# Attention stage rebuilt: one read of V with a shifted copy, 32x32 turns on DVE, the maximum subtracted on PE

## The chip, the cores and the metric

The kernel runs on one core of a Trainium2 chip. A core has five engines with their own instruction streams: PE (matrix multiply, with weight loads), DVE (vector), ACT (scalar functions), POOL (general, here mostly the issue of DMAs) and SP (issue of DMAs); 16 DMA engines move data between DRAM and the on-chip memory SBUF. PE writes to a memory of its own, PSUM, which DVE and ACT read. The metric is the device time in microseconds, the median of the runs; lower is better.

## The reference

Two layers follow each other. First an attention by chunks over q, k, v of shape 4 x 8 x 768 x 64 (batch, head, row, width): each chunk of 32 query rows sees 16 rows to its left, its own 32, 8 to its right, and 8 memory rows of its head, 64 keys in all.

```python
for c in range(nc):                       # 24 chunks of 32 rows
    l_start, r_end = max(0, 32*c - 16), min(S, 32*c + 32 + 8)
    k_full = concat(mem_k, k[l_start:r_end]); v_full = concat(mem_v, v[l_start:r_end])
    scores = (q_c @ k_full.T) / sqrt(64)
    a = exp(scores - max(scores)); a = a / (sum(a) + 1e-9)
    out_c = a @ v_full
```

Its output, 3072 tokens of 512, goes into a mixture of 8 experts: logits and noise logits per token, the two best experts with a softmax over the two, and for each the product `relu(x @ w1[e]) @ w2[e]` (512 to 1024 to 512), weighted and added.

## The kernel before

**Pairs, batches, groups.** The attention runs over 16 head pairs (`NPAIR`; four per batch). A loop of 19 iterations (lines 479 to 519) is a software pipeline written out by hand. Its order is the order of each engine's queue. In iteration i, PE transposes P of pair i-1 (`PT_pe`), multiplies pair i-3 by the router's weights (`logits_pe`), transposes q and k of pair i+2 (`qkT_pe`, 24 matmuls against an identity in four PSUM tiles, evacuated by ACT in four copies), multiplies P of pair i-1 with V (`PV_pe`), makes the scores of pair i+1 (`scores_pe`) and transposes the output of pair i-2 (`xT_pe`). DVE takes the maximum of pair i (`max_dve`), copies the transposed P of pair i-1 from PSUM (`PT_dve`), subtracts the maximum (`sub_dve`, whose exponential is ACT's) and divides the output of pair i-1 (`mult_dve`). The score tile `ps_s` and the output tile `ps_o` have one buffer each, so scores of i+1 wait until those of i have been read, and PV of i-1 waits for `mult_dve` of i-2.

**Scores and PV.** The scores of a pair lie as 128 query rows (four chunks) by six blocks `u` by 64 keys; one bank for each head. `scores_pe` takes 12 matmuls for the memory keys and 48 of 64 rows by 32 columns for the windows. `PV_pe` takes six matmuls of 128 x 128 for the memory rows and a column of ones (which gives the sum for the division), then 24, one per chunk, of 128 rows by 32 columns for both heads together.

**Loads.** All of q, k, v is loaded by POOL, with a cast from fp32 to bf16, in groups of two pairs, three groups deep. V is stored by chunk: 56 partitions hold the window rows of a chunk, so rows that lie in two windows are read twice, in runs of one row (`load_v`, line 121). Loads of a later group stand in the loop behind the work that frees the buffer, and on POOL's queue in the order of the program, among the scatters named next.

**Routing.** When the four pairs of a batch are through the logits, `start_route` puts the route of the batch into a list, of which `steps` runs one entry per iteration: `s1` and `s2` (choice of two experts), then `s3` to `s6`, `s7(0)` and `s7(1)` (each six indirect DMAs on POOL, which scatter the rows of `xrow` with their gates into per-expert lists in DRAM, line 420), and `s8`. Batches 0, 1 and 2 are routed inside the loop, in iterations 7, 11 and 15; batch 3 after it.

**Experts.** From iteration 16 SP loads the rows of the lists transposed (`load_x`; it waits for the scatters of batch 2), and PE runs the up and down products of the eight experts (lines 529 to 701). The results are gathered, added and scattered to the output by indirect DMAs on POOL. An expert list holds up to 832 rows; a loop for rows beyond that is in the program and is not entered by this data.

**Start.** DVE clears three V buffers and `zrow`; ACT issues eight DMAs that write zeros to the ends of the lists, then the four that load `mk_nat` (the memory keys), whose transposes are PE's first work (line 224).

## Time and profile before

| | us |
|---|---|
| runs of the kernel | 442.45, 445.95, 452.03 |
| median | 445.95 |
| profiled execution: its time | 448.12 |
| its span, first to last instruction | 446.4 |
| mean granted PE clock | 0.818 |
| busy: PE, DVE, ACT, POOL | 288.7, 175.6, 108.0, 219.9 |

Lines of the profile name an engine, a line of the kernel, an operation and its tiles (out<-in) with count, busy time and the mean of one in ns, and the idle time before them with what ended it. In the order of time a row begins with its start and its length in us and ends with the idle time before it in brackets; "issue" is idle time for which the profile shows no semaphore. Rows of stretches give start and end, length, busy us of PE, its weight loads, DVE, ACT and POOL, then the granted PE clock, the DMA share and the GB/s moved, counted as written. The strips on the page cut the span in 40 slices of 11.2 us, in tenths.

### The profile page before, as it was taken

What the parts mean: (1) busy time and instruction counts of PE and PEld (TensorE: products, weight loads), DVE (VectorE), ACT (ScalarE), POOL (GpSimd) and SP (SyncE); (2) the same over time, 40 slices, a digit from 0 to 9 for tenths busy, and PEclk for the clock granted to TensorE, in tenths of its full rate; (3) what the DMA queues carried; (4) which work ended last, traced back from release to release, by engine and by line L of the source; (5) the groups of instructions that cost most, each with busy time, mean ns of one, the idle gap of its engine ahead of it and who ended that gap; (6) DMA issues with size and microseconds to landing.
All of it is one profiled execution on the core that took longest, in us unless ns stands there. A gap on an engine that the chain in (4) does not pass through costs nothing. (4 is left out here: it accounts for less than half of the span.)

```text
span 446.4 us, 7962 instructions
## 1 busy us (share of the span) xinstructions
PE 288.7 (65%) x3247; PEld 168.7 (38%) x3257; DVE 175.6 (39%) x403; ACT 108.0 (24%) x202; POOL 219.9 (49%) x245
## 2 busy tenths in 40 slices
PE   0077686527646550595780599869887888979950
PEld 0065565315535430242340254335442443435420
DVE  7234566505632752050220262534623526345230
ACT  1064564306523221142140013013030030301300
POOL 7952341587364036037347152734726717456660
PEclk9998885658555655598895699889998998999995
DMA  9999999139994012515869997595995965943440
GB/s 82 206 167 153 145 107 67 65 100 160 164 212 156 1 46 106 100 42 141 211 141 145 197 209 229 106 245 125 162 222 151 161 182 130 245 128 142 131 159 33
DMA packets 121640, 63.36 MB, mean 142 GB/s; under 512 B 93516, under 2 KB 110940, under 8 KB 121600
## 3 DMA queue, kind: packets, MB, share of 16 engines
q0 software_dynamic: 81488, 54.22, 74.1%
q1 hardware_dynamic: 38672, 7.41, 9.7%
q10 hardware_dynamic: 1440, 1.18, 0.9%
q8 instruction: 27, 0.44, 0.4%
q14 instruction: 13, 0.11, 0.1%
HBM read 69.79 MB, written 21.43 MB: 204 GB/s over the span
## 5 line engine op out<-in xcount | busy, mean ns | idle before, releaser
L604 PE MATMUL ps_y<-w2t,ht 128*128 128x512 bf16 x375 | 92.5, 403 | 31.5 <-DMA w2t<-in_moe_w_dram 17.8
L590 POOL DMA_INDIRECT acc<-out_dram,gi x49 | 49.9, 1018 | 64.1 <-issue 60.2
L555 PEld LDWEIGHTS <-w1t 128*128 128x128 bf16 x512 | 50.9, 101 | 75.9 <-issue 39.2
L612 POOL DMA_INDIRECT out_dram<-acc,wi x56 | 55.9, 998 | 44.7 <-DVE acc L610 20.7
L555 PE MATMUL ps_g<-xT,w1t 128*128 128x416 bf16 (+2 forms) x280 | 64.6, 346 | 13.2 <-issue 6.4
L604 PEld LDWEIGHTS <-ht 128*128 128x128 bf16 x384 | 39.3, 103 | 82.8 <-issue 42.4
L555 PE MATMUL ps_h<-xT,w1t 128*128 128x416 bf16 (+2 forms) x231 | 58.6, 359 | 16.7 <-DMA xT<-x_lists 13.2
L610 DVE SCALAR_TENSOR_TENSOR acc<-ps_y,mt,acc 128x512 f32<-128x512 f32 (+1 forms) x49 | 34.0, 695 | 63.4 <-PE ps_y L604 37.9
L420 POOL DMA_INDIRECT x_lists<-xrow,offA x24 | 23.9, 996 | 60.7 <-issue 25.4
L543 ACT ACTIVATE ht<-ps_g 128x416 bf16<-128x416 f32 (+2 forms) x44 | 21.9, 511 | 115.8 <-PE ps_g L555 69.4
L121 POOL DMA_DIRECT2D vg<-in_v_dram x34 | 33.0, 976 | 27.9 <-PE ps_o L307 20.9
L543 ACT ACTIVATE ht<-ps_h 128x416 bf16<-128x416 f32 (+2 forms) x41 | 21.5, 532 | 77.3 <-issue 35.7
L545 DVE TENSOR_SCALAR ht<-ps_g 128x416 bf16<-128x416 f32 (+2 forms) x26 | 15.0, 579 | 38.9 <-PE ps_g L555 27.1
L420 POOL DMA_INDIRECT x_lists<-xrow,offB x24 | 23.9, 996 | 10.8 <-issue 5.5
L265 PE MATMUL ps_s<-kT,qT 64*32 64x56 bf16 (+2 forms) x768 | 14.8, 213 | 21.5 <-issue 20.9
L276 DVE TENSOR_REDUCE mx<-ps_s 128x12 f32<-128x768 f32 x16 | 15.2, 951 | 30.8 <-PE ps_s L268 30.8
L331 ACT COPY xt<-p_x 128x768 bf16<-128x768 bf16 x16 | 12.8, 799 | 54.8 <-PE p_x L329 53.9
L563 DVE MEMSET acc<- 128x512 f32 x49 | 23.8, 485 | 2.9 <-issue 0.3
L243 ACT CAST qT<-p_t 128x384 bf16<-128x384 f32 x32 | 17.2, 596 | 18.0 <-PE p_t L241 17.1
L265 PEld LDWEIGHTS <-qT 64*32 64x32 bf16 x768 | 10.3, 99 | 24.5 <-issue 24.2
L319 DVE RECIPROCAL rec<-ps_o 128x12 f32<-128x12 f32 x16 | 3.7, 233 | 38.7 <-PE ps_o L307 21.7
L243 ACT CAST kT<-p_t 128x384 bf16<-128x384 f32 x32 | 17.1, 612 | 4.7 <-PE p_t L241 4.6
(128 smaller groups left out, 329.2 us busy)
## 6 DMA issues: line engine op xcount, KB each, us to landing
w1t<-in_moe_w_dram POOLq DMA_DIRECT2D x8, 1024.0 KB
w2t<-in_moe_w_dram POOLq DMA_DIRECT2D x8, 1024.0 KB
vg<-in_v_dram POOLq DMA_DIRECT2D x30, 168.0 KB
qg<-in_q_dram POOLq DMA_DIRECT2D x6, 384.0 KB
kg<-in_k_dram POOLq DMA_DIRECT2D x6, 384.0 KB
x_lists<-zrow ACTq DMA_DIRECT2D x8, 136.0 KB
out_dram<-acc,wi POOLq DMA_INDIRECT x56
acc<-out_dram,gi POOLq DMA_INDIRECT x49
```

What stands on the lines that cost most here:

```text
L121: nc.gpsimd.dma_start(out=vg[p0 + j:p0 + j + nj, x, c:c + n, hh, :], in_=bass.AP(v.tensor, v.offset + (hd * S + c * chunk + j - left_ctx) ...
L243: nc.scalar.copy(dst[:, :, SH * x:SH * (x + 1)], p_t.rearrange("d j p -> d p j"))
L265: nc.tensor.matmul(out=o[:, lo:hi], lhsT=qT[hs, chunk * c:chunk * (c + 1)], rhs=kT[hs, k0 + lo:k0 + hi], start=True, stop=True)
L276: nc.vector.tensor_reduce(out=mx, in_=st[n]["ps"], axis=AX, op=Alu.max)
L420: sc = nc.gpsimd.indirect_dma_start(out=xl_part[2 * (t0 + t) + role], out_offset=bass.IndirectOffsetOnAxis(ap=R["off"][role][:, t:t + 1], ...
L543: nc.scalar.activation(out=dst, in_=src, func=Act.Relu)
L555: nc.tensor.matmul(out=ps[x][:, :w], lhsT=W1[e][:, kp, f * 128:(f + 1) * 128], rhs=XT[e][:, kp, lo + x * w:lo + (x + 1) * w], start=(kp == ...
L563: nc.vector.memset(a, 0.0)
L590: nc.gpsimd.indirect_dma_start(out=(a[:, :DH] if last else a).bitcast(I32), out_offset=None, in_=(out_h(out) if last else out).bitcast(I32 ...
L604: nc.tensor.matmul(out=ps_y, lhsT=HT[e][:, f, i * 128:(i + 1) * 128], rhs=W2[e][:, f, :], start=(f == 0), stop=(f == FB - 1))
L610: nc.vector.scalar_tensor_tensor(out=a[:, :w], in0=ps_y[:, :w], scalar=gate, in1=a[:, :w], op0=Alu.mult, op1=Alu.add)
L612: nc.gpsimd.indirect_dma_start(out=out_h(o) if last else o, out_offset=bass.IndirectOffsetOnAxis(ap=IX[e][0][:, i:i + 1], axis=0), in_=a[: ...
```

## The change

The attention stage and its loads are rebuilt; from the logits on, the code is the same, with other line numbers.

- **Layout of keys.** The 64 keys of a chunk are ordered as two halves (even and odd rows) of 28 window positions and 4 memory positions each. V is loaded once per batch into `va`, two rows of V to a partition, 128 partitions a tile, 24 tiles a batch; `vb` is the same shifted by 16 partitions (32 rows), made from `va` by DMAs inside SBUF (`spread_v`, on SP). In both, partitions 28 to 31 of every 32 are overwritten with memory rows from `memst`. A chunk's window then lies in 32 partitions of `va` (even chunks) or `vb` (odd chunks). Columns of ones stand to the left and right of the two rows.
- **Chunks to rows.** The rows of a score tile are chunks `8*(s//2) + 2*r + s%2`, so tokens stand in another order in `xrow`; the noise and the token numbers (`nz_all`, `tok_i`, `part_i`, `tile_i`) are loaded or made in that order.
- **Scores.** Two matmuls per chunk and head (memory 2 x 4 keys, window 2 x 28), 96 a pair, all 64 rows by 32 columns. The maximum is written as bf16 and subtracted by PE: two matmuls of 384 columns with minus the identity add it into the score banks; ACT's exponential reads PSUM.
- **P.** DVE turns P in 32 x 32 blocks in SBUF (`PT_dve`); the six PE transposes and the copy are gone.
- **PV.** 96 matmuls a pair of 32 rows by 32 columns against 65 columns of `va` or `vb`, for each half j; the sum of exponentials is the sum of columns 0 and 65 of each block (a small reduce before the reciprocal).
- **Turns of q and k.** Transposes with bf16 output in one PSUM tile of six, evacuated by one ACT copy each; q's is placed ahead of the maximum's subtraction, k's behind it.
- **Order.** Loads by whole batches, two deep, on POOL: batch 0 in two parts, batch 1 in the prologue, batches 2 and 3 in iterations 2 and 4, 6 and 8. `s7(0)` and `s7(1)` are taken out of the list and put behind `steps`, in iterations 7, 11, 15 and 8, 12, 16. w1 of expert 0 is loaded in iteration 8, w2 of expert 0 in 9, w1 of expert 1 in 12. The zero writes and DVE's constants move into `constants()` in iteration 2, on SP; `mk_nat` is loaded first on ACT's queue.

```diff
...
+        VP, V0 = 160, 16
+        VT = H * S // 256
+        vbufs = [(ap_.tile([128, VT + 1, VP], BF16, name=f"va{i}", bufs=1), ap_.tile([128, VT, VP], BF16, name=f"vb{i}", bufs=1)) for i in range(2)]
...
+        def load_v(b, lo, hi):
+            va, at = vbufs[b % 2][0], v.offset + (b * H * S - left_ctx) * D
...
+            nc.gpsimd.dma_start(out=va[:, lo:hi, V0:V0 + 2 * D], in_=bass.AP(v.tensor, at + 256 * lo * D, [[2 * D, 128], [256 * D, hi - lo], [1, 2 * D]]))
...
+        def spread_v(b, lo, hi):
+            va, vb = vbufs[b % 2]
+            nc.sync.dma_start(out=vb[:112, lo:hi, :], in_=va[16:, lo:hi, :])
+            nc.sync.dma_start(out=vb[112:, lo:hi, :], in_=va[:16, lo + 1:hi + 1, :])
+            for dst in (va, vb):
+                for r in range(4):
+                    nc.sync.dma_start(out=dst[32 * r + 28:32 * r + 32, lo:hi, :], in_=memst[4 * b:4 * b + 4, lo:hi, :])
...
+        load_qk(0, 0, 2)
...
+        load_v(0, 0, 7)
...
+        nc.scalar.copy(memst.rearrange("p (h r) c -> p h r c", h=H)[:, :, :, V0:V0 + 2 * D],
+                       mv_nat.rearrange("p h (o c) -> p h o c", o=1).to_broadcast([B * 4, H, VT // H, 2 * D]))
+        load_qk(0, 2, H)
+        load_v(0, 7, VT)
+        spread_v(0, 0, 6)
...
+        spread_v(0, 6, VT)
...
+        load_qk(1)
+        load_v(1, 0, VT)
+        spread_v(1, 0, VT)
...
+        def constants():
+            for e in range(E):
+                nc.sync.dma_start(out=xl_d[(e + 1) * CAP - 128:(e + 1) * CAP, :], in_=zrow)
...
+        def turn_pe(n, x):
...
+            p_t = psT.tile([128, SJ, 128], BF16, name="p_t", tag="tr")
+            for j in range(SJ):
+                for hh in range(2):
+                    nc.tensor.transpose(out=p_t[64 * hh:64 * hh + 64, j, :], in_=src[:, 2 * hp + hh, j * D:(j + 1) * D], identity=identb)
...
+                nc.scalar.copy(dst.rearrange("d (p j) -> d j p", j=SJ), p_t)
...
-        def sub_dve(n):
-            sd = ap_.tile([128, 2, BT, CTX], F32, name="sd")
-            nc.vector.tensor_tensor(out=sd, in0=st[n]["ps"], in1=bc4(st[n]["mx"], CTX), op=Alu.subtract)
+        def sub_pe(n):
+            for hh in range(2):
+                nc.tensor.matmul(out=st[n]["ps"][:, hh], lhsT=minus, rhs=st[n]["mx"][:, hh, :].rearrange("p (s o) -> p s o", o=1).to_broadcast([128, BT, CTX]),
+                                 start=False, stop=True, skip_group_check=True)
...
-            for u in range(BT):
-                nc.tensor.transpose(out=p_p[:, u, :], in_=P[:, u, :, :], identity=identb)
...
-            nc.vector.tensor_copy(PT, st[n]["p_p"])
+            PT = ap_.tile([128, BT, 2, 2, 32], BF16, name="PT")
+            nc.vector.transpose(out=PT.rearrange("p s h j c -> p (s h j c)"), in_=st[n]["P"].rearrange("p s h c -> p (s h c)"))
...
+            for s in range(BT):
+                for hh in range(2):
+                    t = (2 * hp + hh) * (VT // H) + s // 2
+                    for j in range(2):
+                        for r in range(4):
+                            rs = slice(32 * r, 32 * r + 32)
+                            nc.tensor.matmul(out=po[rs, hh, s * OW + j:s * OW + j + D + 1], lhsT=PT[rs, s, hh, j, :],
+                                             rhs=vbufs[b % 2][s % 2][rs, t, V0 - 1 + j * (D + 1):V0 + D + j * (D + 1)],
+                                             start=(s == 0 and j == 0), stop=(j == 1), skip_group_check=True)
...
+            if i + 2 < NPAIR:
+                turn_pe(i + 2, 0)
             if i < NPAIR:
                 max_dve(i)
+                sub_pe(i)
             if i + 2 < NPAIR:
-                qkT_pe(i + 2)
+                turn_pe(i + 2, 1)
...
+            steps(1)
+            if i in (2, 6):
+                load_qk(i // 4 + 2)
+            if i in (4, 8):
+                load_v(i // 4 + 1, 0, VT)
+                spread_v(i // 4 + 1, 0, VT)
+            if i in (7, 11, 15):
+                done[i // 4 - 1]["s7"](0)
+            if i == 8:
                 load_w1(0)
+            if i == 9:
                 load_w2(0)
+            if i == 12:
                 load_w1(1)
-            steps(1)
+            if i in (8, 12, 16):
+                done[i // 4 - 2]["s7"](1)
```

## The prediction

> **What bounds the kernel now.** I read the page first, for the stages.

> ```profile
> span 446.4 us, 7962 instructions
> ...
> PEclk9998885658555655598895699889998998999995
> DMA  9999999139994012515869997595995965943440
> ...
> q8 instruction: 27, 0.44, 0.4%
> ...
> L604 PE MATMUL ps_y<-w2t,ht 128*128 128x512 bf16 x375 | 92.5, 403 | 31.5 <-DMA w2t<-in_moe_w_dram 17.8
> ...
> vg<-in_v_dram POOLq DMA_DIRECT2D x30, 168.0 KB
> qg<-in_q_dram POOLq DMA_DIRECT2D x6, 384.0 KB
> ```

> One slice is 11.2 us. For seven slices the DMA engines are full while PE's clock flips between half and full; then comes a hole, a second load burst, and from slice 17 the experts. Then the order of time, from which the pace is read: PE's first work, one maximum per head pair (pairs 0, 2, 5, 6, 8, 9, 12, 13, 15), the third batch's scatter (first and last of 12), and the first expert matmul.

> ```profile
> 23.23 0.60 PE L224 MATMUL p_m<-ident,mk_nat 32*128 32x32 f32 x4 [23.23 <-DMA mk_nat<-in_mem_k_dram]
> 27.01 0.96 DVE L276 TENSOR_REDUCE mx<-ps_s 128x12 f32<-128x768 f32 x1 [12.99 <-PE ps_s L268]
> 37.58 0.95 DVE L276 TENSOR_REDUCE mx<-ps_s 128x12 f32<-128x768 f32 x1
> 58.11 0.95 DVE L276 TENSOR_REDUCE mx<-ps_s 128x12 f32<-128x768 f32 x1
> 63.14 0.95 DVE L276 TENSOR_REDUCE mx<-ps_s 128x12 f32<-128x768 f32 x1
> 81.19 0.95 DVE L276 TENSOR_REDUCE mx<-ps_s 128x12 f32<-128x768 f32 x1
> 99.60 0.96 DVE L276 TENSOR_REDUCE mx<-ps_s 128x12 f32<-128x768 f32 x1 [11.95 <-PE ps_s L268]
> 123.28 0.95 DVE L276 TENSOR_REDUCE mx<-ps_s 128x12 f32<-128x768 f32 x1
> 134.58 0.96 DVE L276 TENSOR_REDUCE mx<-ps_s 128x12 f32<-128x768 f32 x1 [3.53 <-PE ps_s L268]
> 153.85 0.95 DVE L276 TENSOR_REDUCE mx<-ps_s 128x12 f32<-128x768 f32 x1
> 161.78 0.98 POOL L420 DMA_INDIRECT x_lists<-xrow,offA  x1 [17.16 <-DVE base L431]
> 176.28 0.98 POOL L420 DMA_INDIRECT x_lists<-xrow,offB  x1 [0.31 <-issue]
> 183.31 0.58 PE L555 MATMUL ps_h<-xT,w1t 128*128 128x512 bf16 x1 [13.22 <-DMA xT<-x_lists]
> ```

> Four things. PE starts at 23.23, waiting for mk_nat, whose DMAs stand behind eight zero writes on ACT's queue. Pairs 2 to 6 take 25.6 us, 6.4 each; the undisturbed step 58.11 to 63.14 takes 5.0. Two steps are far longer: 18.4 and 11.3 us. And attention hands over through one chain: the scatter of batch 2 begins 7.9 us after the last maximum, lasts 15.5, and 6 us later the experts start. Their 263 us are untouched. So what attention gains or loses by pair 15 reaches the end one for one. The long steps are read next:

> ```profile
> 82.05 1.12 POOL L420 DMA_INDIRECT x_lists<-xrow,offA  x1 [12.80 <-issue]
> ...
> 87.83 0.27 PE L265 MATMUL ps_s<-kT,qT 64*32 64x56 bf16 x5 [1.16 <-issue]
> ...
> 96.39 0.98 POOL L420 DMA_INDIRECT x_lists<-xrow,offB  x1 [0.30 <-issue]
> ...
> 111.22 0.50 PE L265 MATMUL ps_s<-kT,qT 64*32 64x56 bf16 x43 [2.08 <-issue]
> ```

> While Pool scatters (82.05 to 97.4), PE gets its matmuls in handfuls with gaps of 1.2 us that no semaphore explains, until the maximum of 99.60, about 2 us after the scatter. Elsewhere there are single gaps, as the 2.1 us at 111.22. As built, PE's program has 7,211 rows and the instruction queue moved 27 packets: one per 267 rows. A pair issues 272 rows, and such a gap comes at most once in a pair. I take both kinds to be PE waiting for its program, whose packets pass the same DMA engines.

> **The change part by part.** Prices of one operation:

> ```profile
> L281 DVE TENSOR_TENSOR sd<-ps_s,mx 128x768 f32<-128x768 f32 x16 | 15.2, 948 | 0.0
> L295 DVE COPY PT<-p_p 128x768 bf16<-128x768 bf16 x16 | 8.8, 551 | 1.4 <-PE p_p L290 1.4
> L320 DVE TENSOR_TENSOR xrow<-ps_o,rec 128x768 bf16<-128x768 f32 x16 | 15.3, 957 | 1.1 <-POOL xrow L315 0.4 <-DVE rec L319 0.2
> L319 DVE RECIPROCAL rec<-ps_o 128x12 f32<-128x12 f32 x16 | 3.7, 233 | 38.7 <-PE ps_o L307 21.7 <-remote 13.9 <-PE p_x L329 3.1
> L243 ACT CAST qT<-p_t 128x384 bf16<-128x384 f32 x32 | 17.2, 596 | 18.0 <-PE p_t L241 17.1 <-issue 0.9
> L331 ACT COPY xt<-p_x 128x768 bf16<-128x768 bf16 x16 | 12.8, 799 | 54.8 <-PE p_x L329 53.9 <-PE p_p L290 0.9
> ...
> 59.65 0.53 PE L241 MATMUL p_t<-identb,qg 128*64 128x128 bf16 x12
> 61.43 0.52 PE L307 MATMUL ps_o<-vg,PT 128*32 128x128 bf16 x24
> 62.17 0.51 PE L265 MATMUL ps_s<-kT,qT 64*32 64x56 bf16 x40
> 73.36 0.99 PE L241 MATMUL p_t<-identb,kg 128*64 128x128 bf16 x12 [0.36 <-ACT qT L243]
> 75.98 0.83 PE L307 MATMUL ps_o<-vg,PT 128*32 128x128 bf16 x24
> ...
> 10.00:20.00 10.00, 0.00 (x0) 0.00 (x0) 3.48 (x19) 0.00 (x0) 8.09 (x10) 1.00 1.31 194
> 23.20:80.00 56.80, 42.63 (x1163) 34.64 (x1164) 29.78 (x52) 31.33 (x59) 20.62 (x24) 0.82 1.62 123
> ```

> *Start and loads.* mk_nat goes ahead of the zero writes, which move to SP at pair 2, behind the copies; PE can then begin near 12 us (the va memsets, and the ACT copy that fills memst, stand before it). That lead does not last. Pair 2's iteration opens with transposes of pair 4, which need q and k of batch 1. One tensor's batch is 0.79 MB in bf16 (8 heads x 768 x 64 x 2 B). Ahead stand q, k, v of batch 0, the copy vb with its memory rows (1.2 MB) and q, k of batch 1: 5.1 MB. At 123 and at 194 GB/s (last column) that is 26 to 42 us. V's runs double in length and V falls from 5.4 MB (30 issues of 168 KB, the first and the last head's beside them) to 3.1, so I take 185: 28 us plus 2 before the first issue. Pair 2 at 30 instead of 37.6: **-7.6**, range -9 to +6.

> *The pair.* DVE loses the 0.95 subtraction and the 0.55 copy and gains a transpose of 768 elements and a small reduce (0.23, as the reciprocal). No row shows the transpose. The copy of the same tile, 0.55, bounds it below; above I allow the reduce with half as much again, 1.4; I take the 0.95 of the reduce, which also walks 768 elements one by one. DVE: 3.64 to 3.3 us. ACT evacuates q and k in two copies of about 0.9 (row L331, some more for the stride) instead of four of 0.6, and reads the scores from PSUM for the exponential; it stays below 4 us. PE's 24 PV matmuls of 128 columns, four beside each other, took 0.52 at full clock (row 61.43, "warm") and 0.83 at half (75.98, "cold"); six over the full width stream as many columns and cost the same. So before, PV (six and 24) and six transposes each of P and xT cost four times that. Now PV is 96 of 65 columns, each worth 0.51 (columns) to 0.61 (with the 32 weight columns) of one of the 24: 1.1 to 1.3 us warm, 1.7 to 2.0 cold. The transposes of P go. Scores become 96 instead of 60, at 40 in 0.51 less the last one's passage of some 0.15 (an estimate): 0.85 instead of 0.55. Subtracting the maximum costs two of 384 columns; L604's 375 of 512 took 0.25 each, so 0.37 warm, 0.7 cold. With the 24 q and k transposes (1.06 warm, 1.7 cold without the tails) PE's work beside the logits is 4.0 us warm (3.7 before) and 6.0 cold (5.6). Order matters more: the subtraction no longer covers PV on DVE. The loop is maximum 0.95, transpose 0.95, PV 1.2, reduce, reciprocal and product 1.42, hand-overs 0.3 (an estimate): 4.8; through PE 4.0 plus the logits, which wait for the copy of xt (0.8): 4.9. So **4.9 us** against 5.0, range 4.5 (a 0.55 transpose) to 7.0 (all at half clock, 6.0 plus 1.0). From pair 2 to 6 the load pace goes too: 25.6 us become 4 x 5.1 plus what follows, 22.6: **-3**, range -7 to +6. For the nine steps after pair 6, about 0.4 each off the loaded, half-clock ones: **-4**, range -9 to +15.

> *PE's program.* It grows to 10,347 rows: 12 more packets, 464 rows or 1.7 packets a pair. A boundary costs between nothing and the 2.1 us of 111.22; about half of the added ones fall in loaded time. I take 0.8 for five: **+4**, from 0 to 12 x 2 = 24. [...]

> *Scatters.* The step of 18.4 us and the three from 123.28 to 153.85 take 49 us, some 25 more than four at 6. Now the two roles of batches 0 and 1 are scattered an iteration apart, with load_v(3) and load_w1(0) in front of the second; load_v(3) waits for PV of pair 7, which is in PE's slow time. More program per pair means that PE runs dry sooner in each window: **+2**, from -6 to +10. In exchange no q, k or V load stands behind a scatter any more. Batch 2's scatter now overlaps the last PV (192 rows), covered by the chain above that waits for the scatter anyway; uncovered it would be 3.

> *Moved at no cost:* constants() puts 11 DVE operations of some 0.2 us and eight zero writes into pair 2, where PE waits for q and k; the writes stand on SP behind spread_v(1) and must only precede the first scatter. SP's eight noise pieces and ten copies per piece of V are waited for only by PV and the route of pair 6; PV(0) may wait for them, hidden by the 30 us. W1 and W2 are issued earlier, the experts need them after 160 us.

> **Sum:** -7.6 - 3 - 4 + 4 + 2 = -8.6. The profiled execution took 448.1 us (446.4 span and 1.7 around it), the median of the runs is 446.0; I put the sum on the median: **437 us**.

> **The rivals.**

> A, a *larger gain* (423). PE becomes denser, keeps full clock, the transpose is as cheap as the copy, the program gaps go with the load. Start -9, pairs 2 to 6 -7, then -7: -23. For it: 5.0 us in a stretch at full clock. Against: loads last until pair 8 in both.

> B, *no net change* (446). The start lead is real but boundaries (+8) and scatter windows (+6) take it back; the same stall, later.

> C, *slower: PE becomes the bound at half clock* (461). A pair then costs PE 7.0 us with the logits' wait, against 6.4 in the four loaded steps and 5.4 in nine (the undisturbed 5.0, and some allowance for half clock). It decides from about 5.7 us a pair on: 4 x 0.6 + 9 x 1.6 = +17, program +4, scatter +2, start -7.6: +15. The clock decides:

> ```profile
> 100.07 0.85 PE L290 MATMUL p_p<-identb,P 128*128 128x128 bf16 x6
> ...
> 99.60:103.10 3.50, 3.19 (x42) 2.61 (x40) 2.38 (x3) 1.90 (x4) 3.50 (x6) 0.51 1.18 175
> 103.10:106.50 3.40, 2.79 (x116) 2.30 (x116) 2.12 (x4) 2.37 (x4) 3.34 (x4) 1.00 2.17 148
> ```

> A full window (3.19 of 3.50 busy) brings the clock from 0.51 to 1.00, and in that window PE ran transposes among others, those of P in the first row. [...] The window went to full clock with them, so I keep C small.

> [...]

> **How the numbers follow.** Forecast 0.40 (428 to 446), A 0.22, B 0.13, C 0.18, D 0.07. What a measurement can tell from no change is 2%, here 9 us: below 437 is faster, over 455 slower. Half of the forecast and all of A: faster 0.42. The other half and most of B: same 0.31. C, D and a little of B: 0.27. The range leaves out D and the tails of A and C: 420 to 463.

> **What would show it.** First PE work near 12 us, the third maximum near 30; steps of about 5 us where nothing is scattered; 39 instruction packets; PV's 96 within 1.3 us at full clock; the clock of pairs 2 to 8 above 0.8; first expert matmul near 175. The prediction is wrong if PV takes over 3 us, if the steps are 7 us at half clock, or if the two scatter windows of one batch cost more than 20 us together.

## The result, and the profile after

The changed kernel takes 477.8 us (median of four runs, 476.4 to 480.5) against 445.2 for the kernel before: a ratio of 1.076, with a 95% interval of 1.068 to 1.085. It is slower by 32.6 us, where 437 was forecast. In two later groups of runs it came out at 1.066 and 1.069. The profiled execution took 480.5 us.

First the landmarks of the changed kernel in order of time (start, duration, engine, line): PE's first work, the maxima of pairs 0, 2, 6 and 15, and the first expert matmul.

```profile
8.15 0.31 PE L226 MATMUL p_m<-ident,mk_nat 32*128 32x32 f32 x1 [8.15 <-DVE ident L188]
...
15.70 0.96 DVE L274 TENSOR_REDUCE mx<-ps_s 128x12 bf16<-128x768 f32 x1 [7.43 <-PE ps_s L268]
37.53 0.96 DVE L274 TENSOR_REDUCE mx<-ps_s 128x12 bf16<-128x768 f32 x1 [4.83 <-PE ps_s L268]
73.04 0.96 DVE L274 TENSOR_REDUCE mx<-ps_s 128x12 bf16<-128x768 f32 x1 [4.82 <-PE ps_s L268]
187.68 0.95 DVE L274 TENSOR_REDUCE mx<-ps_s 128x12 bf16<-128x768 f32 x1
...
217.38 0.58 PE L555 MATMUL ps_h<-xT,w1t 128*128 128x512 bf16 x1 [0.46 <-DMA xT<-x_lists]
```

Set beside the rows of before: the first maximum comes 11.3 us earlier (15.70 for 27.01), that of pair 2 at the same time (37.53 for 37.58), that of pair 6 is 9.9 late (73.04 for 63.14), that of pair 15 33.8 late (187.68 for 153.85), the first expert matmul 34.1 late (217.38 for 183.31). The experts take 261 us for 263. So the whole loss arises between the first maximum and the last, and there it is 45.1 us, since the start gained 11.3.

What fills those stretches? The view of busy time by stretches, summed from the first maximum to the last in five pieces, before and then after (length, then each engine's busy time):

```profile
sum 126.84, PE 80.26 PEld 62.92 DVE 62.16 ACT 53.54 POOL 58.20; mean PE 16.05 PEld 12.58 DVE 12.43 ACT 10.71 POOL 11.64
```

```profile
111.72:150.47 38.75, 21.16 (x731) 15.80 (x729) 14.32 (x41) 18.74 (x17) 8.64 (x11) 0.50 0.72 131
...
sum 171.98, PE 92.45 PEld 67.87 DVE 58.48 ACT 82.61 POOL 34.49; mean PE 18.49 PEld 13.57 DVE 11.70 ACT 16.52 POOL 6.90
```

PE is busy 12.2 us longer, and in the stretch shown the column after the busy times (PE's granted clock) stands at half, as in the one ahead of it and, at 0.55, the one behind it. By the trace's records of the clock PE had full clock for 37 of the 127 us before and for 10 of the 172 after. ACT is busy 29 us longer, DVE 4 less. PE idles 79.5 us for 46.6. The view of PE's waits says on what (sum, number of times, longest). Before, from 8 to 160 us:

```profile
PE ps_s L265 <- issue: 20.9, 23, 2.1
...
PE p_t L241 <- issue: 3.3, 2, 1.9
PE ps_s L268 <- issue: 1.6, 2, 1.2
...
PE ps_s L255 <- issue: 0.9, 2, 0.5
```

After, from 8 to 190 us:

```profile
PE ps_o L300 <- issue: 18.5, 28, 2.1
PE ps_s L279 <- DVE mx L274: 15.7, 8, 5.6
PE ps_s L264 <- issue: 11.4, 5, 4.7
PE ps_s L262 <- issue: 8.8, 5, 5.0
PE ps_l L334 <- ACT xt L326: 8.7, 10, 0.9
...
PE ps_s L262 <- ACT P L282: 6.8, 5, 3.6
```

This gives the budget of the 45.1 us:

| first to last maximum, us | before | after | difference |
|---|---|---|---|
| PE busy | 80.3 | 92.5 | +12.2 |
| PE waits that no semaphore explains ("issue") | 26.7 | 38.7 | +12.0 |
| the subtraction on PE waits for DVE's maximum | 0 | 13.3 | +13.3 |
| scores wait until the exponential has read their banks | 0 | 6.8 | +6.8 |
| the rest | 19.9 | 20.7 | +0.8 |

(Of the 15.7 us that the view gives for the subtraction, one wait of 2.5 lies behind the last maximum.) The third and the fourth row are new waits, which the change makes. Before, DVE subtracted: it read the scores, freed their banks, and PE never waited for it there. Now PE itself subtracts, in its own queue: what stands behind the two matmuls of L279, the other transposes, PV and the next scores, waits with them for the maximum. The stretch around pair 7 shows it:

```profile
85.00 0.22 PE L264 MATMUL ps_s<-kT,qT 64*32 64x56 bf16 x1 [4.73 <-issue]
...
86.21 0.80 ACT L326 COPY xt<-p_x 128x768 bf16<-128x768 bf16 x1 [5.66 <-PE p_x L324]
87.15 0.24 ACT L353 ACTIVATE ns<-ns 128x48 f32<-128x48 f32 x1
...
87.43 0.21 DVE L358 TENSOR_TENSOR nl<-ns,nz_all 128x48 f32<-128x48 f32 x1 [6.42 <-DMA va<-memst]
...
89.85 0.95 DVE L274 TENSOR_REDUCE mx<-ps_s 128x12 bf16<-128x768 f32 x1
...
90.86 0.80 PE L279 MATMUL ps_s<-mx,minus 128*128 128x384 bf16 x2 [1.75 <-DVE mx L274]
```

Scores of pair 7 come 4.73 us late out of a stall of PE and are done at 85.3. DVE could take their maximum then, but ahead of it in its queue stands the router's L358, which waits for ACT's second router activation (L353), which stands behind the copy of xt, which stands behind PE's stalled scores. (The view puts this wait down to a DMA, whose data had long been there; it is the activation that came last.) The maximum comes 4.5 us late, and now PE stands too. Before, the same order of the router cost DVE 3.0 us too, but PE met DVE's delays there only as waits for PT, 2.7 us between the first and the last maximum, and for the router's nl, 4.1 (5.7 after); they are in the table's rest.

The stalls themselves fall on boundaries of the program. I counted PE's rows in the trace up to each long gap, and took the packets of the instruction queue from its DMA records:

```
         PE stands         rows so far   packet of the instruction queue
after    32.03 to 37.06       961        34.65 to 35.62
after    68.94 to 72.34      2753        70.10 to 71.07
after    80.28 to 85.00      3265        82.46 to 83.71
before   46.36 to 47.79       961        44.88 to 45.76
before  109.14 to 111.22     3009       107.97 to 109.56
```

The prices of single operations, from the groups by line:

```profile
L242 ACT COPY qT<-p_t 128x768 bf16<-128x768 bf16 x16 | 43.5, 2721 | 24.3 <-PE p_t L239 24.3
L246 ACT COPY kT<-p_t 128x768 bf16<-128x768 bf16 x16 | 23.4, 1465 | 0.0
L287 DVE STREAM_TRANSPOSE PT<-P 128x768 bf16<-128x768 bf16 x16 | 15.5, 968 | 0.0
...
133.70:135.40 1.70, 1.50 (x96) 1.34 (x96) 0.50 1.03 142
```

The instruction queue moved 40 packets (39 were expected). The transpose costs 0.97. PV's 96 matmuls take 1.50 us at half clock (last row). The copies of the turned q and k cost 2.72 and 1.46, where 0.9 each was expected.

### The profile page after: what moved, and what is told of

The parts are those of the page before. It is cut to its first block, busy times and chain, and to the rows that moved or that the text cites. A ratio compares the mean times of both kernels' runs of the same rounds, so it can differ in the third digit from the quotient of the medians.

```text
span 478.8 us, 11140 instructions
## 1 busy us (share of the span) xinstructions
PE 303.1 (63%) x4815; PEld 174.3 (36%) x4825; DVE 167.8 (35%) x406; ACT 141.6 (30%) x171; POOL 189.1 (40%) x216
## 4 chain that ended last, share of the span: by engine, by line
DMA 25%; issue 24%; PE 22%; POOL 10%; DVE 7%; SPq 4%; ACT 3%; another core or an unknown queue 1%; POOLq 0%; DVEq 0%; ACTq 0%
DMA out_dram<-acc,wi 10%; PE ps_y L604 8%; DMA vb<-va 6%; POOL out_dram L612 4%; DMA acc<-out_dram,gi 4%; PE ps_o L300 3%; DMA x_lists<-xrow,offB 3%; POOL x_lists L415 3%; PE ps_g L555 2%; SPq L124 2%; POOL acc L590 2%; PE ps_s L264 2%; PE p_t L239 2%; PE p_x L324 1%; DMA vb<-memst 1%
## 5 line engine op out<-in xcount | busy, mean ns | idle before, releaser
L604 PE MATMUL ps_y<-w2t,ht 128*128 128x512 bf16 x375 | 91.3, 399 | 33.5 <-DMA w2t<-in_moe_w_dram 20.4
L590 POOL DMA_INDIRECT acc<-out_dram,gi x49 | 49.8, 1016 | 64.6 <-DMA out_dram<-acc,wi 33.8
L555 PEld LDWEIGHTS <-w1t 128*128 128x128 bf16 x512 | 51.1, 101 | 62.6 <-issue 25.9
L612 POOL DMA_INDIRECT out_dram<-acc,wi x56 | 55.9, 998 | 41.7 <-DVE acc L610 20.5
L555 PE MATMUL ps_g<-xT,w1t 128*128 128x416 bf16 (+2 forms) x280 | 64.4, 346 | 10.5 <-issue 4.9
L604 PEld LDWEIGHTS <-ht 128*128 128x128 bf16 x384 | 38.9, 102 | 83.9 <-issue 43.3
L555 PE MATMUL ps_h<-xT,w1t 128*128 128x416 bf16 (+2 forms) x231 | 58.9, 362 | 5.5 <-issue 4.1
L543 ACT ACTIVATE ht<-ps_g 128x416 bf16<-128x416 f32 (+2 forms) x44 | 21.7, 511 | 117.9 <-PE ps_g L555 77.0
L242 ACT COPY qT<-p_t 128x768 bf16<-128x768 bf16 x16 | 43.5, 2721 | 24.3 <-PE p_t L239 24.3
L300 PEld LDWEIGHTS <-PT 32*32 32x32 bf16 x1536 | 24.5, 119 | 42.4 <-issue 36.9
L326 ACT COPY xt<-p_x 128x768 bf16<-128x768 bf16 x16 | 12.8, 798 | 82.2 <-PE p_x L324 62.0
L300 PE MATMUL ps_o<-vb,PT 32*32 32x65 bf16 x768 | 24.9, 235 | 16.6 <-issue 14.0
L313 DVE TENSOR_REDUCE rec<-ps_o 128x12 f32<-128x24 f32 x16 | 2.9, 182 | 89.6 <-PE ps_o L300 56.7
L300 PE MATMUL ps_o<-va,PT 32*32 32x65 bf16 x768 | 23.7, 235 | 15.7 <-issue 9.9
L262 PE MATMUL ps_s<-mkT,qT 64*32 64x8 bf16 x768 | 17.8, 181 | 18.7 <-issue 8.8
L264 PE MATMUL ps_s<-kT,qT 64*32 64x56 bf16 (+2 forms) x768 | 18.2, 202 | 12.5 <-issue 11.4
L274 DVE TENSOR_REDUCE mx<-ps_s 128x12 bf16<-128x768 f32 x16 | 15.2, 953 | 27.3 <-PE ps_s L268 27.2
```

The costliest lines, as they stand in the source:

```text
L242: nc.scalar.copy(dst.rearrange("d (p j) -> d j p", j=SJ), p_t)
L262: nc.tensor.matmul(out=o[:, :, 28:], lhsT=qT[hs, chunk * c:chunk * (c + 1)], rhs=mkT[hs, hp, b], start=(s == 0), stop=False, skip_group_ch ...
L264: nc.tensor.matmul(out=o[:, :, lo:hi], lhsT=qT[hs, chunk * c:chunk * (c + 1)], rhs=kT[hs, :, k0 + lo:k0 + hi], start=False, stop=False, sk ...
L274: nc.vector.tensor_reduce(out=mx, in_=st[n]["ps"], axis=AX, op=Alu.max)
L300: nc.tensor.matmul(out=po[rs, hh, s * OW + j:s * OW + j + D + 1], lhsT=PT[rs, s, hh, j, :], rhs=vbufs[b % 2][s % 2][rs, t, V0 - 1 + j * (D ...
L543: nc.scalar.activation(out=dst, in_=src, func=Act.Relu)
```

## The experiments

The kernels ran in five groups, each group on one chip together with the kernel before. The kernel before took 448.6, 442.2, 449.5, 443.2 and 447.7 us in them. In groups one, three and five, and in both first profiles, PE got its program in handfuls while Pool scattered; in two and four, in no kernel. Group five ran on the same chip as group four. So ratios are compared within a group, or between groups of one kind; the section on the unexpected comes back to this.

**Group one: single suspects.** First the copies of ACT, whose loops run the other way:

```diff
-nc.scalar.copy(dst.rearrange("d (p j) -> d j p", j=SJ), p_t)
+nc.scalar.copy(dst.rearrange("d (p j) -> d p j", j=SJ), p_t.rearrange("d j p -> d p j"))
...
-nc.scalar.copy(dst.rearrange("d y (p a) -> d a y p", a=SJ // 2), p_t.rearrange("d (a y) p -> d a y p", y=2))
+nc.scalar.copy(dst.rearrange("d y (p a) -> d y p a", a=SJ // 2), p_t.rearrange("d (a y) p -> d y p a", y=2))
```

> The changed kernel, with one thing altered: the two copies that evacuate the turned q and k walk in the order of their destination (PSUM is read with a stride, SBUF is written in a row) instead of the other way round. In the changed kernel the copy of qT takes 2.72 us and that of kT 1.46. Theory ACT (the ring of a pair is maximum, subtraction on PE, exponential, next scores, because one pair of PSUM banks holds the scores until the exponential has read them; the exponential stands behind the copy of qT on ACT): each copy falls to 0.8 to 1.2 us, each step that is not set by a load or a scatter loses 1.5 to 1.9 us, ten of the fifteen steps do: 478 becomes 459 (455 to 465). Theory program (the steps are long because PE waits for its program, 10,347 rows): the copies fall as much, the steps hardly, 474 or more. If the copies stay above 2 us, the stride of the destination is not what makes them slow.

Measured: 480.4 us, ratio 1.069 (1.062 to 1.077). Its groups by line and its waits of PE:

```profile
L242 ACT COPY qT<-p_t 128x768 bf16<-128x768 bf16 x16 | 12.8, 798 | 27.4 <-PE p_t L239 27.4
L246 ACT COPY kT<-p_t 128x768 bf16<-128x768 bf16 x16 | 12.8, 798 | 2.4 <-PE p_t L239 2.4
```

```profile
PE ps_s L279 <- DVE mx L274: 16.9, 8, 5.8
PE ps_o L300 <- issue: 15.3, 31, 1.2
PE ps_s L264 <- issue: 13.1, 8, 4.7
PE ps_s L262 <- issue: 10.4, 5, 6.5
```

Both copies fall to 0.80, 2.6 us less a pair, and the wait of scores for the exponential is gone. The total does not move. The maximum of pair 2 comes 3.6 us earlier (33.9), that of pair 3, behind V, 2.1, that of pair 6 0.6 (72.4), and then nothing is left; the waits for program (38.8 in the three rows) and for the maximum stay. A step without load or scatter, from pair 4 to 5, went from 7.3 to 6.9 us. The theory of ACT on the ring falls: PE's own work is as long with its waits. In the changed kernel it is 92.45 us in 15 steps or 6.2 us a step, and at half clock more (20.12 us in the three steps from 73.04, 21.16 in the three from 111.72, or 6.7 and 7.1 a step).

Second, both scatters of a batch in one iteration:

```diff
                 done[i // 4 - 1]["s7"](0)
+                done[i // 4 - 1]["s7"](1)
...
-            if i in (8, 12, 16):
-                done[i // 4 - 2]["s7"](1)
```

> The changed kernel, with the two scatters of one batch issued in the same iteration (7, 11, 15), ahead of the load of V of batch 3 and of the expert weights. Theory order (the first product of batches 2 and 3 waits for the row buffer until the second scatter has landed, 10 us after its last issue behind V and weights): the step from the maximum of pair 9 to that of pair 10, 19.6 us, falls to about 10, total 478 to 468 (463 to 473). Theory trickle (while Pool scatters, PE gets its program in handfuls, whatever the order): the two windows of some 7.5 us become one of 15, total within 4 us of 478.

Measured: 484.8 us, 1.081 (1.072 to 1.090). The maximum of pair 10 came at 126.1 instead of 131.3, as the first theory had it, but that of pair 9 had come 7.5 us late (119.2 for 111.7), behind both halves in one window, and that of pair 11 was late again (143.3 for 141.0): PE stood 5.1 us at a boundary of its program in the scores of pair 11, while the copies of V of batch 3 ran, whose load now stood behind twelve scatters instead of six. Moving a stretch in a full queue moved the wait. The total is on the side of the trickle's theory, though above its range (474 to 482); the ratio is that of the changed kernel within the intervals.

Third, V read from DRAM twice:

```diff
+            nc.gpsimd.dma_start(out=vb[:, lo0:hi - last, V0:V0 + 2 * D], in_=bass.AP(v.tensor, at + (256 * lo0 + 32) * D, ...))
...
-            nc.sync.dma_start(out=vb[:112, lo:hi, :], in_=va[16:, lo:hi, :])
-            nc.sync.dma_start(out=vb[112:, lo:hi, :], in_=va[:16, lo + 1:hi + 1, :])
```

> The changed kernel, with the shifted copy of V read from DRAM as V itself is, instead of copied from SBUF to SBUF; the memory rows are written as before. Theory chain of V (load, copy, memory rows stand one behind another, 30 us for batch 2; PV of pair 1 waits for it until 47.0): PV of pair 1 is done before 40, the maximum of pair 3 comes at 42 instead of 49.7, and the copies of batches 2 and 3 no longer load the engines while PE wants its program: 478 becomes 468 (462 to 474). Rival (the queue that casts takes 0.79 MB more per batch at 120 to 200 GB/s, ahead of q and k of the next batch): 4 to 6 us later for each batch, 480 to 488.

Measured: 490.2 us, 1.090 (1.082 to 1.098): slower, as the rival had it, and 2 us above its range. The maximum of pair 3 came at 52.8 instead of 49.7. Not all of that is V: the edit also clears both `vb` on DVE ahead of the start, and the first maximum came at 20.5 instead of 15.7. That lag had shrunk to 1.9 us at pair 7; the loss arose in the step from pair 9 to 10 (24.7 us for 19.6), where V of batch 3 is loaded. The shifted copy in SBUF is the better of the two.

Fourth, half of PV:

```diff
-                    for j in range(2):
+                    for j in range(1):
```

> The changed kernel with half of PV left out: only the even rows of V are weighted and summed, 48 matmuls a pair instead of 96; PE's program falls from 10,347 to 8,811 rows. Theory program: half of the 1,536 added PV matmuls' rows are gone, and with them half of the excess of the PV that fell into scatter windows (7.6, 7.4, 11.4 and 9.4 us for what takes 1.5 elsewhere, 30 us in excess): 13 to 20 us less, 460 (456 to 466). Theory ACT: PE loses 0.7 us of work in a pair, little of it on the ring: 473 (470 to 477).

Measured: 468.1 us, 1.044 (1.036 to 1.051), between the two theories' ranges and 10 us below the changed kernel's 478 (it took 477.8 to 478.8 in its three groups). Its waits of PE, and its busy time from the first maximum to the last:

```profile
PE ps_s L264 <- issue: 10.7, 11, 1.2
...
PE ps_s L262 <- issue: 5.6, 9, 1.2
PE ps_o L300 <- issue: 5.5, 8, 2.4
...
PE p_x L324 <- issue: 2.8, 1, 2.8
```

```profile
15.69:174.28 158.59, 84.18 (x2732) 0.52 0.74 128
```

The waits for program fall from 38.7 to 24.6, the longest from 5.0 to 2.8; PE's busy time falls by 8.3. That is 22 us of PE's time, for 13.4 from the first maximum to the last in the same two profiles (171.98 to 158.59; the profiled execution, 464.6, was the fastest of its four): what is taken away is partly waited for elsewhere. Rows and PE time fall together here, so this run alone does not tell them apart.

**Group two: the clock, and the rows or the time.**

```diff
-nc.tensor.transpose(out=p_t[64 * hh:64 * hh + 64, j, :], in_=src[:, 2 * hp + hh, j * D:(j + 1) * D], identity=identb)
+nc.tensor.matmul(out=p_t[64 * hh:64 * hh + 64, a, :], lhsT=src[:, 2 * hp + hh, j * D:(j + 1) * D], rhs=identb, start=True, stop=True)
```

> The changed kernel, with q and k turned as in the kernel before: matmuls against the identity into f32 PSUM in halves, four copies of some 0.6 us on ACT, written in a row, in place of PE's transposes and two copies. PE's program keeps its 10,347 rows. In the changed kernel the granted clock is half until 62.6 us, full to 69.5, half to 175.3; before it was full for 7 of the 12 windows from 38 to 82.6 and from 103 to 113. Theory clock (24 transposes a pair in the place of matmuls keep PE's clock down; at half clock PE's own order, 6.8 us of transposes, subtraction, PV and scores, is the pair's pace): the granted clock is full for half of 30 to 110 us or more, undisturbed steps fall from 7 to about 5, total 478 to 458 (450 to 466). Theory wait (the clock follows how much PE waits, whatever it runs): the clock stays at half, 474 to 480.

Measured: 465.2 us, 1.055 (1.049 to 1.060). No run of the changed kernel itself exists in a group of this kind, so the size of the gain is open. The theory had full clock for half of 30 to 110 us or more; it came to full in eight single windows of 3.4 us from the first maximum to the last, 27 of 164 us, and stood at half in the long stretches.

The opposite test on the kernel before is the clean one, with the same edit the other way round:

> The kernel before with one part of the change alone: q and k are turned by PE's transposes into bf16 PSUM (still in halves, four copies) in place of matmuls against the identity into f32. Theory clock: it loses the windows of full clock between 38 and 69 and at 103 to 113; its steps there go from 5.0 to 6.5, total 446 to 456 (451 to 465). Theory wait: the clock windows stay, total 443 to 449.

Measured: 443.1 us, 1.003 (0.999 to 1.006). With 24 transposes a pair in the place of matmuls, the kernel before keeps its time and its clock; the view by stretches:

```profile
58.80:72.40 13.60, 8.71 (x298) 1.00 1.75 136
```

Four windows in a row at full clock, 31 us in all from the first maximum to the last. For the kernel before, the theory that transposes hold the clock down falls.

PV narrowed instead of halved:

```diff
-out=po[rs, hh, s * OW + j:s * OW + j + D + 1], ... rhs=...[rs, t, V0 - 1 + j * (D + 1):V0 + D + j * (D + 1)]
+out=po[rs, hh, s * OW + 33 * j:s * OW + 33 * j + 33], ... rhs=...[rs, t, V0 - 1 + 97 * j:V0 + 32 + 97 * j]
```

> The changed kernel with half of PV left out in another way: all 96 matmuls of a pair are issued, each over 33 columns in place of 65, so that 32 of the 64 columns of a head sum the even rows alone and 32 the odd ones. PE's time for PV falls as where half of the matmuls were left out, its program keeps 10,347 rows. That run took 464.6 on the scale of 477.8 (ratio 1.0436). Theory program: nothing or little is gained here, 474 to 478, since the rows were the cost. Theory PE time: the same as there, 463 to 467.

Measured: 462.8 us, 1.048 (1.041 to 1.055). It was meant to stand beside the halved PV, but that ran in a group of the other kind. Against the matmul turn of its own group it is 2.4 us faster. As to the time, inconclusive. Two things can be read from its trace. Its single stalls at the program reach 5.1 us, as in the changed kernel, where halved PV had 2.8 at most; that speaks for the rows rather than PE's time, though the two ran in groups of different kinds. And it keeps the transposes and had one window of full clock, where the matmul turn had eight; so whether the transposes share in the low clock of the changed kernel stays open.

The start alone, on the kernel before:

```diff
-        for e in range(E):
-            nc.scalar.dma_start(out=xl_d[...], in_=zrow)
         mk_nat = ...
         for b in range(B):
             nc.scalar.dma_start(out=mk_nat[...], in_=...)
+        for e in range(E):
+            nc.scalar.dma_start(out=xl_d[...], in_=zrow)
```

> The kernel before with the loads of mem_k ahead of the eight zero writes on the queue of ACT, nothing else. My prediction's term for the start: PE begins near 12 us in place of 23.2, pair 2's maximum comes at 30 in place of 37.6, 7.6 us less in all: 438 (434 to 442). Rival (the pace of pairs 0 to 5 is that of the loads of q and k, as the changed kernel had it, with the maximum of pair 2 at 37.5 after a first one at 15.7): the maximum of pair 0 at 16, that of pair 2 at 35 or later, total 443 to 448.

Measured: 441.8 us, 0.997 (0.993 to 1.000), 0.4 us less than the kernel before in this group, where 7.6 less was forecast. The rows of the maxima of pairs 2 and 7 in this kernel:

```profile
33.32 0.95 DVE L276 TENSOR_REDUCE mx<-ps_s 128x12 f32<-128x768 f32 x1
71.83 0.95 DVE L276 TENSOR_REDUCE mx<-ps_s 128x12 f32<-128x768 f32 x1
```

In the kernel with transposes, which starts as before, they stand at 37.49 and 72.49. The lead is 4.2 us at pair 2 and 0.7 at pair 7: loads and the router take it back.

**Group three: the changed kernel again, row buffers, no copies of V.**

> The changed kernel itself, unaltered, so that the other kernels of this call have it on the same chip. On the chip of the first experiments (before at 448.6) PE got its program in handfuls in every scatter window; on that of the second (442.2) in none, in none of the four kernels. If the handfuls are a matter of the chip, the ratio is 1.05 to 1.065 on one without them and 1.07 to 1.08 on one with them; if they are a matter of the kernel, it is 1.07 to 1.08 on either.

Measured: 478.8 us, 1.066 (1.058 to 1.074), with handfuls: no test of the first alternative.

```diff
-    xp = ctx.enter_context(tc.tile_pool(name="xp", bufs=2))
+    xp = ctx.enter_context(tc.tile_pool(name="xp", bufs=4))
```

> The changed kernel with four buffers for the rows of tokens in place of two, so that the first products of batches 2 and 3 wait for no scatter. In the runs of the second call the product of pair 8 came 19 us after its PV (108.6 to 127.9) and that of pair 12 came 9 us after it, each when the scatter of two batches earlier had landed. Theory wait for rows: both go, the longest steps (23.6 and 14.0 there) fall below 10: 15 us or more less than the changed kernel in this call (12 to 22). Rival (the scatters themselves, on Pool, are the longest chain; the wait only covers it): 5 us or less.

Measured: 478.6 us, 1.067 (1.059 to 1.076): the rival. The wait itself went: the maximum of pair 10 came at 123.9 instead of 130.7, and PE's wait for maxima fell from 16.1 to 10.1 us. One pair later all was as before (140.5 for 140.1): PE stood 1.7 and 3.5 us at two boundaries of the program, the second in the scores of pair 11, and then came the router's activation.

> The kernel before with the same four buffers, nothing else. On the second chip its steps 9 to 10 and 13 to 14 took 14.6 and 21.9 us, each behind a product that waited for its row buffer. Theory wait for rows: 0.965 of the kernel before (0.95 to 0.98). Rival as above: 0.99 to 1.0.

Measured: 449.2 us, 1.000 (0.996 to 1.004). No gain alone here either. But this group has handfuls; without them the kernel before waits longer behind its row buffers (group four), and there the four buffers alone were not run.

```diff
-            nc.sync.dma_start(out=vb[:112, lo:hi, :], in_=va[16:, lo:hi, :])
-            nc.sync.dma_start(out=vb[112:, lo:hi, :], in_=va[:16, lo + 1:hi + 1, :])
```

> The changed kernel without the copies of V from SBUF to SBUF: the second buffer holds the memory rows and otherwise zeros, so the odd tiles of each head sum their memory rows alone; all else is issued as before. Theory load (the copies fill the DMA engines while PE wants its program and the next loads; scores of pairs 2, 6 and 7 took 6, 4.5 and 5.8 us in place of 1, and PV of pair 1 waited until 47.0 us): pair 3's maximum at 43 or earlier in place of 49.7, pair 8's at 90 in place of 100, 10 us less in all than the changed kernel in this call (7 to 14). Rival (any load does it, and the loads of q, k and V alone set these times): 4 us or less.

Measured: 475.2 us, 1.059 (1.051 to 1.067), 3.6 us less than the changed kernel in this group: the rival. Pair 3's maximum came at 48.1 (47.8 there), pair 8's at 97.2 (99.5). This edit too clears both `vb` at the start, which put the first maximum at 20.8 (15.9 there); how much of these 4.9 us reaches the end is not known, so the copies may cost more than 3.6.

**Group four: rows added to the kernel before, and waits taken away together.**

```diff
-matmul(out=ps[:, hh, u * CTX + WIN:...], lhsT=qT[hs, 128 * u:128 * (u + 1)], rhs=mkT[...])
+for r in range(4):
+    matmul(out=ps[32 * r:32 * r + 32, hh, u * CTX + WIN:...], lhsT=qT[hs, 128 * u + 32 * r:128 * u + 32 * r + 32], rhs=mkT[...])
...
-matmul(out=pv[:, u // UB, u % UB], lhsT=PT[:, u, :], rhs=memv[:, n], ...)
+for r in range(4):
+    matmul(out=pv[32 * r:32 * r + 32, u // UB, u % UB], lhsT=PT[:, u, 32 * r:32 * r + 32], rhs=memv[:, n], ...)
```

> The kernel before with 1,728 rows more in PE's program (8,939 in place of 7,211) and the same work: the matmuls of the memory keys and of the memory values over 128 output rows are issued as four over 32 rows, side by side. Theory rows: the stalls at page boundaries, 10 us between the first and the last maximum, double, and the ratio is 1.025 (1.012 to 1.04). Theory load or PE time (the rows as such are hidden): 1.0 to 1.006.

Measured: 447.1 us, 1.010 (1.006 to 1.013), between the two. PE's waits in it:

```profile
PE ps_s L266 <- issue: 13.4, 6, 4.8
...
PE ps_o L306 <- DVE PT L296: 9.1, 5, 3.9
...
PE ps_s L256 <- issue: 4.9, 2, 3.1
...
PE ps_o L309 <- issue: 1.8, 1, 1.8
```

and in the kernel with transposes of group two (also without handfuls, with the 7,211 rows of before):

```profile
PE ps_o L303 <- DVE PT L294: 21.3, 4, 16.3
...
PE p_t L241 <- issue: 2.2, 2, 1.3
```

With the smaller rows that the views leave out, the waits for program from the first maximum to the last are 21.0 us against 3.8, with stalls of up to 4.8, for the same products in 1,728 more rows (PE's busy time rises too, from 75.3 to 80.5). So rows make stalls. But the total rises by 4 only; PE's wait behind the row buffers falls from 21.3 to 9.1, as if the new stalls stood where PE would have waited anyway.

The router's activations at the head of the iteration:

```diff
-            pending.append((r["s1"], r["s2"]))
+            r["s1"]()
+            pending.append((r["s2"],))
```

> The kernel before with the router's two activations of batches 0 to 2 issued on ACT right behind their logits, at the head of the iteration in place of its end. DVE waited 3.0 us for them (68.3 to 71.3) with the maximum of pair 7 queued behind, whose scores were ready at 69.2. Theory order on DVE: 2.9 us less for each of three batches, the first of them hidden by loads: ratio 0.985 (0.978 to 0.993). Rival (PE's program and the scatters set these steps): 0.996 to 1.003.

Measured: 439.7 us, 0.989 (0.982 to 0.997): the theory's order, at the small end.

The three edits together on the kernel before (mem_k first, four row buffers, activations early):

> The kernel before with three edits together: mem_k ahead of the zero writes, four row buffers, the router's activations at the head of the iteration. Each of the first two alone gave 0.997 and 1.0, as another wait took over. If the waits stand in for one another, the three together give more than their sum: 0.975 (0.96 to 0.985). Rival (the scatters on Pool and the loads are the chain): 0.99 to 1.0.

Measured: 428.1 us, 0.965 (0.957 to 0.973). **This version beats both kernels.** Alone the edits gave 0.3, 0.0 (in a group with handfuls) and 1.1%; together 3.5%. That the waits stood in for one another, as expected, is one reading. The other is that four row buffers are worth more without handfuls: PE's wait behind PT, from the first to the last maximum, is 18.4 us in the kernel with transposes, against 2.7 in the profile of the kernel before, and 0.5 here. No run tells the two apart. Its last maximum stands at 129.8 (153.85 in the kernel before) and its first expert matmul at 168.47 (183.31):

```profile
168.47 0.58 PE L556 MATMUL ps_h<-xT,w1t 128*128 128x512 bf16 x1 [15.72 <-DMA xT<-x_lists]
```

The changed kernel with ACT's copies turned, four row buffers and early activations:

> The changed kernel with the copies of ACT walked in the order of the destination, four row buffers and the router's activations at the head of the iteration. Alone the first two gave nothing on chips where the changed kernel had 1.066 to 1.076. If the waits stand in for one another: 1.045 (1.035 to 1.055). If PE's program and its time at half clock are the chain: 1.06 or more.

Measured: 449.2 us, 1.013 (1.004 to 1.021), below both ranges. That looked like most of the loss regained, but the changed kernel itself had no run in such a group.

**Group five: the same kernel beside the changed one.**

> The changed kernel unaltered, beside the version with three edits on the same chip. On a chip with handfuls in the scatters: 1.066 to 1.076 of the kernel before, as twice. On one without: 1.055 to 1.067, since the kernels before and after both lose some 6 us there.

Measured: 477.8 us, 1.069 (1.063 to 1.075), with handfuls, on the chip of group four.

> The changed kernel with the three edits again (copies of ACT walked in the order of the destination, four row buffers, the router's activations at the head of the iteration). Theory waits stand in for one another: 20 us or more below the changed kernel of this call (ratio between the two 0.945 to 0.96), though two of the three alone gave 0 to 3. Theory chip: most of 1.0125 was the chip, 8 us or less.

Measured: 471.5 us, 1.054 (1.049 to 1.060), a ratio of 0.987 to the changed kernel: 6.3 us less, the second theory. Its waits of PE:

```profile
PE ps_s L264 <- issue: 18.1, 8, 5.7
PE ps_o L300 <- issue: 13.5, 28, 1.2
PE ps_l L334 <- ACT xt L326: 11.6, 13, 0.9
PE ps_s L262 <- issue: 10.7, 7, 6.1
...
PE ps_s L279 <- DVE mx L274: 6.4, 5, 1.8
```

Of the two new waits of 22.5 us (15.7 and 6.8 in the view of the changed kernel), 6.4 are left; the waits for program rose from 38.7 to 46 (with two small rows more), those for xt from 8.7 to 11.6. With handfuls, what is taken from the other waits goes in part to PE's program.

## Why the prediction was wrong

*Start and loads, -7.6.* PE began at 8.15 (12 forecast), the first maximum at 15.70, but pair 2's at 37.53 instead of 30: the term was 0. The step that failed is "Pair 2 at 30": I let only the loads gate pair 2. In its way stood a stall of 2.15 us in PV of pair 0, the exponential of pair 0 behind the copy of 2.72 (PE waited 3.6 us for it), and 5.04 us of waiting for program in the scores of pair 2. And a lead there is worth little by itself: on the kernel before it gave 0.3%.

*The pair, 4.9 against 5.0.* The prices were right in part: transpose 0.97 (0.95), PV at half clock 1.50 (1.7 to 2.0), PE's work at half clock 6.7 and 7.1 with the logits (6.0 without). One was far off: ACT's two copies, 4.2 us for 1.8, but the run that took 2.6 of it away moved nothing. What failed first is the choice of the price: the 4.9 us took PE's work at full clock, "through PE 4.0", and from the first maximum to the last PE had full clock for 10 of 172 us. What failed next is the loop itself, "maximum 0.95, transpose 0.95, PV 1.2, reduce, reciprocal and product 1.42": I added up durations and left out the queue. The subtraction stands in PE's queue, and I wrote what it no longer covers on DVE, but not what stands behind it on PE when the maximum is late. These are the 13.3 us, and 6.8 more because the banks of the scores are now free only after the exponential. The steps without load and scatter took 5.9 to 7.3 us; from pair 2 to 6 it was 35.5 us instead of 22.6.

*PE's program, +4 (0 to 24).* The mechanism was right and the size three times too small: 12.0 us more of waiting, with single stalls of 5.0 us where I had 2.1 as the worst and 0.8 as the mean. Adding 1,728 rows to the kernel before shows rows making stalls: 21.0 us of waits for program against 3.8 in the kernel with transposes.

*Scatters, +2.* The gaps of PE in the scatter windows, counted row by row, add up to 19.2 us after (101 to 123 and 151 to 169) and 20.1 before (82 to 100 and 127 to 145), so the 12 us more of waiting for program lie outside them. Putting the halves together did not help. The term's size is not separable from the other waits in these steps.

*Moved at no cost:* not wholly. PE waited 4.0 us in PV of pair 1 for the memory rows that SP's small DMAs write into `va` and `vb` (41.6 to 45.3), inside the long step from pair 2 to pair 3. The other moves no run tested.

*The rivals.* C had the right mechanism (half clock from pair 6 on, "a pair then costs PE 7.0 us") and the right side; at 461 it was 17 us short: it had neither the new waits behind the subtraction (20.1 us in the budget) nor stalls of 5 us. The transposes, at which C looked too, showed no effect in the kernel before (1.003, with its windows of full clock). Why the changed kernel's clock stays low is open. D, with its chance of 0.07, was a PV whose matmuls run one at a time. No run shows that: PV's 96 matmuls in 1.50 us are 62 ns for each four, no more than 65 columns of a single one take at that clock (68, by the subtraction's 0.80 us for twice 384). So four row tiles run side by side here. A and B fell with the start and the pair.

*What is shown and what is not.* Shown: the loss lies before the experts; the budget by PE's time and waits; rows make program stalls. Taken alone and with handfuls, turning ACT's copies, leaving out V's copy, four row buffers and putting the scatters together each gained 4 us or less; the transposes cost nothing in the kernel before. Not settled: how the 45 us divide among subtraction, rows and clock, since each wait that was taken away was partly replaced by another; and why PE's clock is lower. A version with the subtraction back on DVE and all else as changed was not run.

## What to carry to other kernels

When an operation moves to another engine, write down what is queued behind it there and how late its input can be, before adding up durations: here the subtraction, in PE's queue, waited 13.3 us for its maximum. Many small matmuls cost program as well as columns: 1,728 more rows for the same products made 17 us of waits for program, though only 4 us of them reached the total. A null result of one edit does not show that its wait is harmless: three edits that gave 0 to 1% alone gave 3.5% together, whether because waits stand in for one another or because one of them was tried alone in a group of the other kind.

## What the runs showed that was not expected

*Handfuls come and go with the group, not with the chip.* The same kernel (three edits on the changed one) took 449.2 us in group four and 471.5 in group five on the same chip. In its first scatter window PE got through 234 matmuls in group four and 84 in group five (the view by stretches of each; PE's busy time, matmuls in brackets, clock, DMA share, GB/s):

```profile
96.60:104.20 7.60, 6.35 (x234) 0.50 0.27 96
```

```profile
98.20:105.80 7.60, 4.12 (x84) 0.50 0.26 94
```

The DMA engines were equally loaded (0.27 and 0.26), so load does not explain it. What does is open. The kernel before differs by 4 to 7 us between the two kinds of group.

*A copy's price hangs on the order in which it writes.* 768 elements of two bytes cost ACT 2.72 us when each write lies 12 bytes from the last, 1.46 at 6 bytes, and 0.80 when it writes in a row and reads PSUM at a stride of 256 bytes (q) or 512 (k) instead. The strided reads of PSUM show no price here: the copy of xt, which has no such stride, takes 0.80 too. Why the strided writes cost more was not shown.

*The clock's strip shows full before its first record.* In the page of the changed kernel the strip reads 9 for the first 70 us. But one matmul of the subtraction took 0.50 us at 58.2, where the strip says 9, and 0.34 at 64.9, after the first recorded change:

```profile
58.20 0.50 PE L279 MATMUL ps_s<-mx,minus 128*128 128x384 bf16 x1
...
64.86 0.34 PE L279 MATMUL ps_s<-mx,minus 128*128 128x384 bf16 x1
```

So durations, not the strip, tell the clock of the opening stretch. The same holds before: its first record is at 38.2, and the six transposes of P took 0.82 us at 32.0 and 0.50 at 63.0. The full clock that the prediction's rows of stretches show up to there is not measured.
